# Layer 3's projections in half-array products, the lower half two products behind the upper, and key-value sums four tiles at a time

## The chip, the cores and the metric

The kernel runs on one NeuronCore of a Trainium2 chip. The metric is the device time of one execution in microseconds. TensorE is written PE, its weight loads PEld, VectorE DVE, ScalarE ACT, GpSimd POOL, and SyncE, which issues the DMAs, SP.

## The reference

Four layers run one after the other on x of 2048 tokens by 576 features: a linear attention (A), an MLP (B), the same attention again and the same MLP again. Layers 1 and 3 are A, layers 2 and 4 are B. Each adds its result to x.

```python
def _A_ref(x, wqkv, wo):                 # H = 32 heads of Dh = 18
    qkv = (x @ wqkv) ...                 # q, k, v: 2048 x 576 each
    phi = lambda t: jnp.where(t > 0, t + 1, jnp.exp(t)) + 1e-6
    pq, pk = phi(q), phi(k)
    kv = jnp.einsum("bhsd,bhse->bhde", pk, v)
    z = jnp.einsum("bhsd->bhd", pk)
    num = jnp.einsum("bhqd,bhde->bhqe", pq, kv)
    den = jnp.einsum("bhqd,bhd->bhq", pq, z)[..., None] + 1e-6
    return (num / den) ... @ wo

x = x + _A_ref(_layernorm(x), wqkv, wo)
x = x + _B_ref(_layernorm(x), w1, b1, w2, b2)    # layer norm, 576 -> 4608, gelu, -> 576
x = x + _A_ref(_layernorm(x), wqkv, wo)
x = x + _B_ref(_layernorm(x), w1, b1, w2, b2)
```

## The kernel before, in words

**Tiles.** The 2048 tokens are 16 tiles of 128 (`t`), or four chunks of 512 (`c`). The 576 features are contracted in `KD` = 5 steps of 128 rows, so the fifth step holds 64 real rows; its other 64 rows of `wqkv_sb` are zero. The layer norm's result lies turned in `yT` (features down, tokens across). The 32 heads are in five groups `g` of 126 columns (the last: 72).

**Layer A's projection stage** (`layer_A`, the loop at L486). For each tile it issues:
- `k_proj` (L435): two halves of 288 columns, each five full-array products into a buffer of its own from `ps_h`, then phi. `phi_from_psum` (L375) reads PSUM twice on ACT (exp L381, identity L382) and ends with two DVE operations on SBUF (L383, L385). In layer 3 the second half goes by `phi_by_dve` (L366): exp on ACT (L368), then DVE, whose last operation (L371) reads PSUM too. The result is `pk`.
- `v_proj` (L448): two groups of five products, 252 columns (L454) and 324 columns (L457), into the two banks of one `v_ps` tile under the tag accB. ACT copies both halves' first 252 columns at once (L459), DVE the last 72 (L464; ACT, L462, in the first two tiles), into one of two `v_ring` buffers.
- `kv_acc` (L467) of the tile before: five products that add pk and v into `kvacc`, under the tag accA, over all tiles.
- From tile 2 on (layer 3) one `q_proj` (L475): five products of 512 columns, then phi with the columns turned back into order. Twenty such (g, c) pieces are needed; those left over follow behind the loop and between the output products.

**PSUM.** There are eight banks: `ps_h` has four buffers of one bank; accA and accB are one buffer of two banks each. A tile's buffer is released when all that read it are done.

**Order of the work.** A scheduler orders each engine's instructions; on PE, `pe()` (L141) links every product to the last, so PE's order is the order of the code. Each engine then works its list in order. DMAs are issued by SP in its own order. `pre_a1(t)` gives the layer-norm pipe one tick per tile (`LNPipe.tick`, L276): statistics on DVE, the root on POOL (L309), the norm on DVE into one of three `y_ring` buffers, a DVE transpose, DMAs to DRAM and back into `yT` (`land`, L242). In layer 3 this carries the last tiles of the layer before.

**Half-array products** exist already in layer B (`m1_group`, L625): a product of 64 rows on the upper half of the array and one on the lower half go out in turn. Two halves may not write one PSUM bank at the same time, so a block's first lower product waits for a small copy on ACT (a relay, L671) that waits for its last upper product.

Of the kernel before, what the change touches and what calls it, by code (L numbers as in the profile page):

```python
# [9 lines left out]
BF16 = mybir.dt.bfloat16  # L10
F32 = mybir.dt.float32
PSUM = bass.MemoryType.PSUM
DRAM = bass.MemoryType.DRAM

S, D, F, H, DH = 2048, 576, 4608, 32, 18
P = 128
NT = S // P
KD = 5
DPAD = KD * P
NF = F // P  # L20
G = 5
GH = [7, 7, 7, 7, 4]
GR = [h * DH for h in GH]
GO = [126 * g for g in range(G)]
# [4 lines left out]
CA = 512  # L29
NCA = S // CA  # L30
HALF = D // 2
# [3 lines left out]
def build(tc, A_x, A_wqkv, A_wo, B_w1, B_b1, B_w2, B_b2, out, dbg=None, n_layers=4):  # L35
    nc = tc.nc
    dbg = dbg or {}
    with ExitStack() as ctx:
        const = ctx.enter_context(tc.tile_pool(name="const", bufs=1))
        ps_h = ctx.enter_context(tc.tile_pool(name="ps_h", bufs=4, space=PSUM))  # L40
        ps_acc = ctx.enter_context(tc.tile_pool(name="ps_acc", bufs=1, space=PSUM))
# [57 lines left out]
        wqkv_sb = const.tile([P, KD, 3 * D], BF16, name="wqkv_sb")  # L99
# [6 lines left out]
        yT = const.tile([P, KD, S], BF16, name="yT")  # L106
        kvT = const.tile([P, G, 126], BF16, name="kvT")
        zsel = const.tile([P, G, H], BF16, name="zsel")
        NY = 3
        y_ring = [const.tile([P, DPAD], BF16, name=f"y_ring{i}") for i in range(NY)]  # L110
        NV = 2
        v_ring = [const.tile([P, G, P], BF16, name=f"v_ring{i}") for i in range(NV)]
# [6 lines left out]
        blk = ctx.enter_context(tc.tile_pool(name="blk", bufs=NF))  # L119
# [6 lines left out]

        NOSYNC = mybir.DependencyInfo(mybir.DependencyClass.NoSync, mybir.DependencyReason.SCHED_ONLY)
        SYNC = mybir.DependencyInfo(mybir.DependencyClass.Sync, mybir.DependencyReason.DATA)
        relay_sb = const.tile([P, 2], F32, name="relay_sb")
        nc.gpsimd.memset(relay_sb[:], 0.0)  # L130
        chain = dict(last=None)

# [8 lines left out]
        def pe(inst):  # L141
            if pe_chain["on"]:
                if pe_chain["last"] is not None:
                    tc.add_manual_dep(inst.ins, pe_chain["last"], NOSYNC, reason="TensorE order in the MLP")
                pe_chain["last"] = inst.ins.name
            return inst
# [74 lines left out]
        state = dict(ycnt=0, vcnt=0, turns=0)  # L221
# [20 lines left out]
        def land(now=False):  # L242

            for it in list(landing):
                it[0] -= 1
                if it[0] > 0 and not now:
                    continue
                _, home, c, kind = it
                landing.remove(it)
                cols = slice(c * CB, (c + 1) * CB)  # L250
                nc.sync.dma_start(out=yT[:, 0:KD - 1, cols],
                                  in_=home[0:16, :, :].rearrange("(k jj) r n -> (jj r) k n", jj=4))
                for hi in range(2 if kind == "B" else 1):
                    nc.sync.dma_start(out=yT[64 * hi:64 * (hi + 1), KD - 1, cols],
                                      in_=home[16:18, :, :].rearrange("jj r n -> (jj r) n"))

        def spread(ap):

            return ap.rearrange("p (t i c) -> p i t c", t=TPC, i=4)

        def gather(ap):
            return ap.rearrange("p (i t c) -> p i t c", i=4, t=TPC)

        class LNPipe:
            def __init__(self):
                self.items = []
# [88 lines left out]
            def drain(self):  # L355
                while self.items or landing:
                    self.tick()

        lnp = LNPipe()
        act_last = dict(exp=None, gelu=None)  # L360

        def warm_table(func, after):
            warm = nc.scalar.activation(out=act_dummy[:, 0:1], in_=neg_half[:, 0:1], func=func)
            tc.add_manual_dep(warm.ins, after, NOSYNC, reason="table of the next stage loaded early")
# [10 lines left out]
        def phi_from_psum(ps_ap, out_ap, rows, n, turned_cols=False):  # L375
            e = work.tile([P, 512], BF16, name="phi_e", bufs=3)
            a = work.tile([P, 512], BF16, name="phi_a", bufs=2)
            e_out, a_out = e[0:rows, 0:n], a[0:rows, 0:n]
            if turned_cols:
                e_out, a_out, ps_ap = spread(e_out), spread(a_out), gather(ps_ap)  # L380
            act_last["exp"] = nc.scalar.activation(out=e_out, in_=ps_ap, func=ACT.Exp).ins.name  # L381
            nc.scalar.activation(out=a_out, in_=ps_ap, func=ACT.Identity, bias=C1, scale=1.0)  # L382
            nc.vector.tensor_scalar(out=e[0:rows, 0:n], in0=e[0:rows, 0:n], scalar1=1.0, scalar2=1e-6,  # L383
                                    op0=ALU.min, op1=ALU.add)
            top = nc.vector.tensor_tensor(out=out_ap, in0=a[0:rows, 0:n], in1=e[0:rows, 0:n], op=ALU.max)  # L385
            dve_last["phi"] = top.ins.name
# [42 lines left out]
        def layer_A(li, next_kind, pre_a1=None):  # L429
            kvacc = ps_acc.tile([P, 2, 512], F32, name="kvacc", tag="accA")  # L430
            pk_tiles = {}
            v_tiles = {}
            pq = {}
# [41 lines left out]
            def q_proj(g, c):  # L475
# [5 lines left out]
                pq[(g, c)] = blk.tile([P, D], BF16, name="pq", tag="blk")  # L481
                phi_from_psum(qp[0:GR[g], :], pq[(g, c)][0:GR[g], 0:CA], GR[g], CA, turned_cols=(li > 0))

            q_left = [(g, c) for c in range(NCA) for g in range(G)]
            pe_chain["on"] = True
            for t in range(NT):  # L486
                if t != 1 or li > 0:
                    k_proj(t)
                if t == 0 and li == 0:
                    k_proj(1)  # L490
                pre_a1(t)
                v_proj(t)
                if t >= 1:
                    kv_acc(t - 1)
                if t >= (4 if li == 0 else 2):
                    q_proj(*q_left.pop(0))
# [5 lines left out]
                out=kvT[0:127, 0:4, :].rearrange("p g (h e) -> p g h e", h=7),  # L502
# [3 lines left out]
                out=kvT[0:127, 4, 0:72].rearrange("p (h e) -> p h e", h=4),  # L506
# [3 lines left out]
            for g in range(G):  # L510
                pe(nc.tensor.matmul(zp[0:GR[g], g:g + 1], lhsT=kvT[0:127, g, 0:GR[g]], rhs=z_row[0:127, :],
                                 start=True, stop=True))
# [78 lines left out]
            for t in range(NT):  # L591
                c, j = divmod(t, TPC)
# [17 lines left out]
        def next_acc():  # L610
            acc_turn["n"] += 1
            return ("accA", "accB")[acc_turn["n"] % 2]
# [4 lines left out]
        class LayerB:  # L617
# [69 lines left out]

            def run(self):
                li, next_kind = self.li, self.next_kind

                def feed_next(c, i):
                    if c + 1 < NCB:
                        t = (c + 1) * TPC + i
                        lnp.feed(None, t, "B", "dve", "dma", load_from=t, after=dve_last["sum"])

                for c in range(NCB):
                    for g in range(self.done.get(c, 0), NGRP):
                        self.m1_group(c, g)
                        if g in (3, 5):
                            prefetch_xo(li, c * TPC + (g - 3) // 2, add_b2=True)  # L700
                        if g in (2, 3, 4, 5):
                            feed_next(c, g - 2)
                        lnp.tick(transposes=0)
                        lnp.tick(transposes=0)
                    self.flush()
                    if c == NCB - 1 and next_kind == "A":
                        warm_table(ACT.Exp, act_last["gelu"])
                    hT = self.hT.pop(c)
                    for j in range(TPC):
                        t = c * TPC + j  # L710
                        acc = ps_acc.tile([P, 2, 512], F32, name="m2_ps", tag=next_acc())
                        by_half = li == n_layers - 1 and t == NT - 1
                        steps = [(f, half) for half in range(2) for f in range(NF)] if by_half else \
                            [(f, half) for f in range(NF) for half in range(2)]
                        for f, half in steps:
                            pe(nc.tensor.matmul(acc[:, half, 0:HALF], lhsT=hT[f][:, j * P:(j + 1) * P],  # L716
                                                rhs=w2_sb[:, f, half * HALF:(half + 1) * HALF],
                                                start=(f == 0), stop=(f == NF - 1)))
                            if half == 0:
                                continue  # L720
                            if f % 12 == 6:
                                lnp.tick()
                            if f == 18 and j < 2:
                                prefetch_xo(li, c * TPC + 2 + j, add_b2=True)
                        xn = residual(li, t, acc[:, :, 0:HALF])
                        if xn is not None and next_kind == "A":
                            lnp.feed(xn, t, "A", "dve", "dma")
# [40 lines left out]
        for li, kind in enumerate(kinds):  # L768
            nk = kinds[li + 1] if li + 1 < n_layers else None
            if kind == "A":  # L770
                if li == 0:
                    layer_A(li, nk, pre_a1=pre_a1_layer0)
                else:
                    def pre_a1(t):
                        lnp.tick()
# [56 lines left out]
```

## Time and profile before

| | us |
|---|---|
| median of 3 runs | 778.01 (777.93 to 779.69) |
| the profiled execution | 778.13 |
| its span, first to last instruction | 776.4 |
| PE busy | 765.1 |
| ACT busy | 335.4 |
| DVE busy | 276.4 |
| POOL busy | 119.2 |
| layer 3's projections, 393.4 to 451.9 | 58.5 |

The median and the span are not the same measure: the profiled execution took 1.7 us more than its span. In rows of the timeline the columns are start, duration, engine, line, operation, output and inputs, shape, count, and in brackets the idle time before the row and what ended it. Several instructions of a kind are merged into one row, from the first one's start to the last one's end. In the table by stage the columns are the stretch, its length, and busy time with the number of instructions for PE, PEld, DVE, ACT and POOL, then the granted TensorE clock, the DMA engines' share and GB/s.

### The profile page before, as it was taken

What the parts mean: (1) busy time and instruction counts of PE and PEld (TensorE: products, weight loads), DVE (VectorE), ACT (ScalarE), POOL (GpSimd) and SP (SyncE); (2) the same over time, 40 slices, a digit from 0 to 9 for tenths busy, and PEclk for the clock granted to TensorE, in tenths of its full rate; (3) what the DMA queues carried; (4) which work ended last, traced back from release to release, by engine and by line L of the source; (5) the groups of instructions that cost most, each with busy time, mean ns of one, the idle gap of its engine ahead of it and who ended that gap; (6) DMA issues with size and microseconds to landing.
All of it is one profiled execution on the core that took longest, in us unless ns stands there. A gap on an engine that the chain in (4) does not pass through costs nothing.

```text
span 776.4 us, 15770 instructions
## 1 busy us (share of the span) xinstructions
PE 765.1 (99%) x6613; PEld 495.6 (64%) x6613; DVE 276.4 (36%) x711; ACT 335.4 (43%) x738; POOL 119.2 (15%) x185
## 2 busy tenths in 40 slices
PE   7999999999999999999999999999999999999998
PEld 4777664575477457646777766547745764675476
DVE  5786965045113603400355579520140032000000
ACT  4887746403620660164046675561065026304600
POOL 3573312012000301200100004210030011002000
PEclk9999999999999999999999999999999999999999
DMA  8990374106401720230440006730141033011000
GB/s 268 278 296 22 111 242 121 36 31 171 109 16 48 187 61 32 80 75 2 153 100 9 1 2 208 250 81 8 31 128 53 17 124 80 8 32 54 1 11 21
DMA packets 73761, 69.10 MB, mean 89 GB/s; under 512 B 34266, under 2 KB 58330, under 8 KB 73690
## 3 DMA queue, kind: packets, MB, share of 16 engines
q1 hardware_dynamic: 73690, 68.10, 30.2%
q8 instruction: 51, 0.84, 0.5%
q14 instruction: 20, 0.16, 0.1%
HBM read 45.67 MB, written 22.41 MB: 88 GB/s over the span
## 4 chain that ended last, share of the span: by engine, by line
PE 94%; DVE 3%; ACT 1%; issue 1%; POOL 0%; DVEq 0%; ACTq 0%; POOLq 0%
PE m_ps L716 36%; PE h_ps L666 20%; PE hp_ps L666 16%; PE k_ps L441 5%; PE q_ps L478 5%; PE wo_ps L565 4%; PE v_ps L457 3%; PE v_ps L454 2%; PE kvacc L472 1%; PE tp L346 1%; PE warm_ps L176 1%; PE rden_ps L554 1%; ACT rden_bc L556 1%; DVE pq L557 0%; DVE xn L419 0%
## 5 line engine op out<-in xcount | busy, mean ns | idle before, releaser
L716 PE MATMUL m_ps<-w_sb,hT 128*128 128x288 bf16 x2304 | 283.6, 286 | 0.0
L716 PEld LDWEIGHTS <-hT 128*128 128x128 bf16 x2304 | 224.8, 98 | 59.8 <-issue 3.4
L666 PEld LDWEIGHTS <-w_sb 64*128 64x128 bf16 x2304 | 124.6, 94 | 136.4 <-issue 1.9
L666 PE MATMUL hp_ps<-yT,w_sb 64*128 64x512 bf16 x1152 | 178.0, 376 | 0.0
L666 PE MATMUL h_ps<-yT,w_sb 64*128 64x512 bf16 x1152 | 148.0, 376 | 0.0
L671 ACT COPY relay_sb<-relay_sb 128x1 f32<-128x1 f32 x144 | 28.5, 198 | 264.7 <-PE h_ps L666 222.2
L309 POOL TENSOR_TENSOR ln_rstd<-ln_u,neg_half 128x1 f32<-128x1 f32 x64 | 36.4, 571 | 483.3 <-DVE ln_u L302 253.0
L662 ACT ACTIVATE hT<-h_ps,b1T 128x512 bf16<-128x512 f32 x144 | 91.0, 683 | 44.4 <-PE h_ps L666 44.4
L662 ACT ACTIVATE hT<-hp_ps,b1T 128x512 bf16<-128x512 f32 x144 | 91.1, 692 | 0.0
L419 DVE TENSOR_TENSOR xbf<-m_ps,xo 128x576 bf16<-128x576 f32 (+1 forms) x17 | 12.2, 721 | 221.4 <-PE m_ps L716 221.4
L419 DVE TENSOR_TENSOR xo<-m_ps,xo 128x576 f32<-128x576 f32 x16 | 12.1, 757 | 180.1 <-PE m_ps L716 180.1
L403 POOL TENSOR_TENSOR xo<-xo,b_bc 128x576 f32<-128x576 f32 x32 | 40.9, 1281 | 101.9 <-DMA xo<-x_d 61.5
L666 PE MATMUL h_ps<-yT,w_tail 64*128 64x512 bf16 x144 | 54.2, 376 | 0.0
L666 PE MATMUL hp_ps<-yT,w_tail 64*128 64x512 bf16 x144 | 54.1, 376 | 0.0
L478 PE MATMUL q_ps<-yT,wqkv_sb 128*126 128x512 bf16 (+1 forms) x200 | 50.0, 382 | 0.0
L565 PE MATMUL wo_ps<-kvwo,pq 126*128 126x288 bf16 (+1 forms) x320 | 43.5, 285 | 2.6 <-DVE xo L419 1.5
L441 PE MATMUL k_ps<-wqkv_sb,yT 128*128 128x288 bf16 x320 | 44.3, 286 | 0.0
L565 PEld LDWEIGHTS <-pq 126*128 126x128 bf16 (+1 forms) x320 | 30.4, 97 | 13.7 <-issue 3.5
L441 PEld LDWEIGHTS <-yT 128*128 128x128 bf16 x320 | 31.0, 98 | 11.4
L666 PEld LDWEIGHTS <-w_tail 64*128 64x128 bf16 x288 | 27.1, 94 | 17.1
L383 DVE TENSOR_SCALAR phi_e<-phi_e 128x288 bf16<-128x288 bf16 (+2 forms) x88 | 26.1, 297 | 25.0 <-ACT phi_e L381 24.9
L381 ACT ACTIVATE phi_e<-k_ps 128x288 bf16<-128x288 f32 x48 | 20.2, 420 | 34.2 <-PE k_ps L441 34.1
(98 smaller groups left out, 631.6 us busy)
## 6 DMA issues: line engine op xcount, KB each, us to landing
xo<-x_d SPq DMA_DIRECT2D x48, 288.0 KB, 3.9
x_d<-xo SPq DMA_DIRECT2D x32, 288.0 KB, 2.3
xl<-x_d SPq DMA_DIRECT2D x24, 288.0 KB, 4.3
y_d<-turned SPq DMA_DIRECT2D x40, 144.0 KB, 3.2
w_sb<-in_B_w_dram SPq DMA_DIRECT2D x6, 864.0 KB, 10.2
yT<-y_d SPq DMA_DIRECT2D x10, 512.0 KB, 4.1
w_sb<-in_B_w_dram SPq DMA_DIRECT2D x9, 512.0 KB, 5.4
x_d<-xn SPq DMA_DIRECT2D x16, 288.0 KB, 2.1
```

The lines of the kernel that those rows point to most:

```text
L309: nc.gpsimd.tensor_tensor(out=rstd[:], in0=it["u"][:], in1=neg_half[:], op=ALU.pow)
L383: nc.vector.tensor_scalar(out=e[0:rows, 0:n], in0=e[0:rows, 0:n], scalar1=1.0, scalar2=1e-6, op0=ALU.min, op1=ALU.add)
L403: nc.gpsimd.tensor_tensor(out=xo[:], in0=xo[:], in1=b2_bc[:], op=ALU.add)
L419: total = nc.vector.tensor_tensor(out=xn[:, cols].rearrange("p (h n) -> p h n", h=nh), in0=ps, in1=xo[:, cols].rearrange("p (h n) -> p h n ...
L441: pe(nc.tensor.matmul(kp[:, 0:HALF], lhsT=yT[:, k, tok], rhs=wqkv_sb[:, k, D + half * HALF: D + (half + 1) * HALF], start=(k == 0), stop=( ...
L457: pe(nc.tensor.matmul(vp[:, 1, 0:324], lhsT=yT[:, k, tok], rhs=wqkv_sb[:, k, 2 * D + 252: 3 * D], start=(k == 0), stop=(k == KD - 1)))
L478: pe(nc.tensor.matmul(qp[0:GR[g], :], lhsT=wqkv_sb[:, k, GO[g]:GO[g] + GR[g]], rhs=yT[:, k, c * CA:(c + 1) * CA], start=(k == 0), stop=(k ...
L565: pe(nc.tensor.matmul(wp[:, half, 0:HALF], lhsT=pq[(g, c)][0:GR[g], j * P:(j + 1) * P], rhs=kvwo[g][0:GR[g], half * HALF:(half + 1) * HALF ...
L662: act_last["gelu"] = nc.scalar.activation(out=to, in_=ps, func=ACT.Gelu_apprx_tanh, bias=b1T[:, f:f + 1], scale=1.0).ins.name
L666: mm = pe(nc.tensor.matmul(dst[n], lhsT=wt, rhs=mv, start=(seen[n] == 0), stop=(seen[n] == 8)))
L671: relay = nc.scalar.copy(out=relay_sb[:, 1:2], in_=relay_sb[:, 0:1])
L716: pe(nc.tensor.matmul(acc[:, half, 0:HALF], lhsT=hT[f][:, j * P:(j + 1) * P], rhs=w2_sb[:, f, half * HALF:(half + 1) * HALF], start=(f == ...
```

## The change

It concerns layer 3 alone (li > 0), apart from a weight load ahead of it.

- A job is one output half or piece: v0 (252 columns), v1 (324), k0, k1 (288 each) and q (512). Each tile adds the jobs q (from tile 2), v0, v1, k0, k1. A job has four upper products (rows 0 to 63 of each 128) and four lower ones; the fifth step, 64 rows, is one product more: on the lower half for v0, v1 and k0, on the upper for k1 and q.
- `RowTiles.add` issues a job's upper products; the lower products of the job two before are queued and put between them, as two counters of columns keep the halves level. A job's first lower product waits for a POOL memset (the relay), which waits for its last upper product. When its last lower product is issued, its copies or phi follow.
- The v tile is one accB buffer with two banks as before (for tile 0, two `ps_h` buffers); its copies by ACT and DVE come when both halves are done.
- `kv_acc`, still in full-array products, comes in groups of four tiles behind tiles 4, 8 and 12, then for tiles 12 to 14 behind the loop. Five v buffers are used: the two of `v_ring` and the three of `y_ring`, whose constant columns POOL sets at tiles 1 to 3.
- The layer-norm pipe gets two ticks per tile, ahead of the tile's products.
- The fifth step's 64 rows of keys' and values' weights are loaded a second time into rows 64 to 127, at the start of layer 2, and `yT`'s last 64 rows too for layer 3, by one more DMA per chunk.
- Behind the loop one q, the sums of tile 15 and another q follow as before.

The core of the diff:

```diff
-                for hi in range(2 if kind == "B" else 1):
+                for hi in range(2):
                     nc.sync.dma_start(out=yT[64 * hi:64 * (hi + 1), KD - 1, cols],
...
+                def v_start(half):
+                    def start():
+                        if t == 0:
+                            tiles[half] = ps_h.tile([P, 512], F32, name="v0_ps", tag="h")[...]
+                        else:
+                            if half == 0:
+                                tiles["v"] = ps_acc.tile([P, 2, 512], F32, name="v_ps", tag="accB")
+                            tiles[half] = tiles["v"][:, half, 0:edges[half + 1] - edges[half]]
...
+                def v_finish(half):
+                    def finish():
...
+                        elif half == 1:
+                            nc.scalar.copy(out=va[:, 0:4, 0:126]..., in_=tiles["v"][:, :, 0:252]...)
+                        if half == 1:
+                            nc.vector.tensor_copy(out=va[:, 4, 0:72], in_=tiles[1][:, 252:324])
...
+            class RowTiles:
+                def ops(self, job, hi):
+                    r = slice(64 * hi, 64 * hi + 64)
+                    return [(job, hi, job["w"](r, k), job["m"](r, k))
+                            for k in range(KD - 1 + (job["tail"] == hi))]
+                def emit(self, op, first, last):
+                    job, hi, w, m = op
+                    mm = pe(nc.tensor.matmul(job["dst"], lhsT=w, rhs=m, start=(first and hi == 0), stop=(last and hi == 1)))
+                    self.at[hi] += job["n"]
+                    if first and hi == 1:
+                        tc.add_manual_dep(mm.ins, job["relay"], SYNC, ...)
+                    if last and hi == 0:
+                        relay = nc.gpsimd.memset(relay_sb[:, 2:3], 0.0)
+                        tc.add_manual_dep(relay.ins, mm.ins.name, SYNC, ...)
+                        job["relay"] = self.relay = relay.ins.name
+                    if last and hi == 1:
+                        job["finish"]()
+                def lower(self, limit):
+                    while self.low and (limit is None or self.at[1] <= limit):
+                        self.emit(*self.low.pop(0))
+                def add(self, job):
+                    if len(self.begun) == 2:
+                        if not self.low:
+                            self.at[1] = max(self.at)
+                        self.queue_lower(self.begun.pop(0))
+                    self.begun.append(job)
+                    job["dst"] = job["start"]()
+                    ops = self.ops(job, 0)
+                    for i, op in enumerate(ops):
+                        self.lower(self.at[0] - 1)
+                        self.emit(op, i == 0, i == len(ops) - 1)
+                def full(self, func):
+                    func()
+                    self.at = [max(self.at)] * 2
...
+            if li > 0:
+                va_ring = v_ring + [... for y in (y_ring[(state["ycnt"] + i) % NY] for i in range(NY))]
+                stream = RowTiles()
+                for t in range(NT):
+                    pre_a1(t)
+                    pre_a1(t)
+                    if t in (1, 2, 3):
+                        va = va_ring[t + 1]
+                        for part, value in ((va[:, 4, 72:126], 0.0), (va[:, :, 126:127], 1.0), (va[:, :, 127:128], 0.0)):
+                            init = nc.gpsimd.memset(part, value)
...
+                    if t >= 2:
+                        stream.add(q_job(*q_left.pop(0)))
+                    for job in half_jobs(t):
+                        stream.add(job)
+                    if t % 4 == 0 and t > 0:
+                        stream.full(lambda: [kv_acc(u) for u in range(t - 4, t)])
+                stream.drain()
+                for u in range(NT - 4, NT - 1):
+                    kv_acc(u)
...
             def run(self):
                 li, next_kind = self.li, self.next_kind
+                if next_kind == "A":
+                    nc.sync.dma_start(out=wqkv_sb[64:P, 4, D:3 * D], in_=A_wqkv[4 * P:D, D:3 * D])
```

More of the change, by code (lines that the diff above doesn't have):

```diff
@@ L128, in build @@
         SYNC = mybir.DependencyInfo(mybir.DependencyClass.Sync, mybir.DependencyReason.DATA)
[L129 removed]
+        relay_sb = const.tile([P, 4], F32, name="relay_sb")
         nc.gpsimd.memset(relay_sb[:], 0.0)
@@ L482, in q_proj, with half_jobs, k_start, start @@
                 phi_from_psum(qp[0:GR[g], :], pq[(g, c)][0:GR[g], 0:CA], GR[g], CA, turned_cols=(li > 0))
+            def half_jobs(t):
+                tok = slice(t * P, (t + 1) * P)
+                tiles = {}
+                va = va_ring[t % len(va_ring)]
+                edges = (0, 252, D)
+                def v_start(half):
+                    def start():
+                        if t == 0:
+                            tiles[half] = ps_h.tile([P, 512], F32, name="v0_ps", tag="h")[:, 0:edges[half + 1] - edges[half]]
+                        else:
+                            if half == 0:
+                                tiles["v"] = ps_acc.tile([P, 2, 512], F32, name="v_ps", tag="accB")
+                            tiles[half] = tiles["v"][:, half, 0:edges[half + 1] - edges[half]]
+                        return tiles[half]
+                    return start
+                def v_finish(half):
+                    def finish():
+                        if t == 0:
+                            nc.scalar.copy(out=va[:, 2 * half:2 * half + 2, 0:126],
+                                           in_=tiles[half][:, 0:252].rearrange("p (g c) -> p g c", g=2))
+                        elif half == 1:
+                            nc.scalar.copy(out=va[:, 0:4, 0:126].rearrange("p (b g) c -> p b g c", b=2),
+                                           in_=tiles["v"][:, :, 0:252].rearrange("p b (g c) -> p b g c", g=2))
+                        if half == 1:
+                            nc.vector.tensor_copy(out=va[:, 4, 0:72], in_=tiles[1][:, 252:324])
+                            v_tiles[t] = va
+                    return finish
+                def k_start(half):
+                    def start():
+                        tiles["k", half] = ps_h.tile([P, 512], F32, name="k_ps", tag="h")[:, 0:HALF]
+                        if half == 0:
+                            tiles["pk"] = blk.tile([P, D], BF16, name="pk", tag="blk")
+                        return tiles["k", half]
+                    return start
+                def k_finish(half):
+                    def finish():
+                        phi = (phi_from_psum, phi_by_dve)[half]
+                        phi(tiles["k", half], tiles["pk"][:, half * HALF:(half + 1) * HALF], P, HALF)
+                        if half == 1:
+                            pk_tiles[t] = tiles["pk"]
+                    return finish
+                def rows_of(cols):
+                    return lambda r, k: wqkv_sb[r, k, cols]
+                y_of = lambda r, k: yT[r, k, tok]
+                jobs = []
+                for half in range(2):
+                    cols = slice(2 * D + edges[half], 2 * D + edges[half + 1])
+                    jobs.append(dict(w=y_of, m=rows_of(cols), tail=1, n=edges[half + 1] - edges[half],
+                                     start=v_start(half), finish=v_finish(half)))
+                for half in range(2):
+                    cols = slice(D + half * HALF, D + (half + 1) * HALF)
+                    jobs.append(dict(w=y_of, m=rows_of(cols), tail=1 - half, n=HALF,
+                                     start=k_start(half), finish=k_finish(half)))
+                return jobs
@@ new lines, in q_job, with start, finish @@
+            def q_job(g, c):
+                hold = {}
+                def start():
+                    hold["q"] = ps_h.tile([P, 512], F32, name="q_ps", tag="h")[0:GR[g], :]
+                    return hold["q"]
+                def finish():
+                    pq[(g, c)] = blk.tile([P, D], BF16, name="pq", tag="blk")
+                    phi_from_psum(hold["q"], pq[(g, c)][0:GR[g], 0:CA], GR[g], CA, turned_cols=True)
+                return dict(w=lambda r, k: wqkv_sb[r, k, GO[g]:GO[g] + GR[g]],
+                            m=lambda r, k: yT[r, k, c * CA:(c + 1) * CA], tail=0, n=CA, start=start, finish=finish)
@@ new lines, in layer_A, with __init__, queue_lower, drain @@
+            class RowTiles:
+                def __init__(self):
+                    self.at = [0, 0]
+                    self.begun = []
+                    self.low = []
+                def ops(self, job, hi):
[7 more added lines that the diff above has]
+                    if first and hi == 1:
+                        tc.add_manual_dep(mm.ins, job["relay"], SYNC, reason="row tiles take turns on a PSUM bank")
+                    if last and hi == 0:
+                        relay = nc.gpsimd.memset(relay_sb[:, 2:3], 0.0)
+                        tc.add_manual_dep(relay.ins, mm.ins.name, SYNC, reason="row tiles take turns on a PSUM bank")
+                        job["relay"] = self.relay = relay.ins.name
[4 more added lines that the diff above has]
+                        self.emit(*self.low.pop(0))
+                def queue_lower(self, job):
+                    ops = self.ops(job, 1)
+                    self.low += [(op, i == 0, i == len(ops) - 1) for i, op in enumerate(ops)]
+                def add(self, job):
[12 more added lines that the diff above has]
+                    self.at = [max(self.at)] * 2
+                def drain(self):
+                    while self.begun:
+                        self.queue_lower(self.begun.pop(0))
+                    self.lower(None)
@@ L484, in layer_A @@
             q_left = [(g, c) for c in range(NCA) for g in range(G)]
             pe_chain["on"] = True
-            for t in range(NT):
-                if t != 1 or li > 0:
+            if li > 0:
+                va_ring = v_ring + [y[:].rearrange("p (g c) -> p g c", g=G) for y in
+                                    (y_ring[(state["ycnt"] + i) % NY] for i in range(NY))]
+                stream = RowTiles()
[3 more added lines that the diff above has]
+                    if t in (1, 2, 3):
+                        assert t < 3 or not lnp.busy()
+                        va = va_ring[t + 1]
+                        for part, value in ((va[:, 4, 72:126], 0.0), (va[:, :, 126:127], 1.0), (va[:, :, 127:128], 0.0)):
+                            init = nc.gpsimd.memset(part, value)
+                            tc.add_manual_dep(init.ins, stream.relay, NOSYNC, reason="relays first")
+                    if t >= 2:
[7 more added lines that the diff above has]
+                    kv_acc(u)
@@ L488, in layer_A @@
+            for t in range(NT if li == 0 else 0):
+                if t != 1:
                     k_proj(t)
-                if t == 0 and li == 0:
+                if t == 0:
                     k_proj(1)
```

## The prediction

> **What bounds the kernel now.** I read the page first: TensorE is busy for nearly the whole span at the full granted clock, and the chain of work that ended last is TensorE.
>
> ```profile
> span 776.4 us, 15770 instructions
> PE 765.1 (99%) x6613; PEld 495.6 (64%) x6613; DVE 276.4 (36%) x711; ACT 335.4 (43%) x738; POOL 119.2 (15%) x185
> ...
> PE 94%; DVE 3%; ACT 1%; issue 1%; POOL 0%; DVEq 0%; ACTq 0%; POOLq 0%
> ```
>
> So the change is worth what it does to TensorE's products and waits in one stage, layer 3's projections. The table by stage cuts it out: from the first k_ps product (393.42) to the first q_ps product behind the token loop (451.93) it is 58.5 us, all of it PE, while ACT is busy for 38.4 and DVE for 33.1.
>
> ```profile
> 393.40:451.90 58.50, 58.50 (x467) 44.26 (x465) 33.09 (x112) 38.35 (x92) 0.55 (x1) 1.00 0.13 32
> ```
>
> The timeline of PE over one token tile shows products back to back. A row is a run of products: its length less that of one, over the count less one, is the step from product to product.
>
> ```profile
> 423.20 0.85 PE L457 MATMUL v_ps<-wqkv_sb,yT 128*128 128x324 bf16 x5
> 423.89 0.42 PE L472 MATMUL kvacc<-pk,v_ring 128*128 128x126 bf16 x5
> 424.15 1.26 PE L478 MATMUL q_ps<-yT,wqkv_sb 128*126 128x512 bf16 x5
> 425.25 1.39 PE L441 MATMUL k_ps<-wqkv_sb,yT 128*128 128x288 bf16 x10
> 426.48 0.70 PE L454 MATMUL v_ps<-wqkv_sb,yT 128*128 128x252 bf16 x5
> ```
>
> With one product's 271, 286 and 300 ns (252, 288, 324 columns) the steps are 107, 122.5 and 137.5 ns; 512 columns take 216. One tile with q is 3.81 us (k_ps at 425.25 and, a tile earlier, 421.44).
>
> **The gain: fewer products.** The MLP already works in half-array products. Its timeline gives their step: from one w_tail row to the next like it lie 18 half products, nine pairs, in 1.94 us, so a pair takes 215.6 ns, as long as one full product.
>
> ```profile
> 265.13 0.38 PE L666 MATMUL h_ps<-yT,w_tail 64*128 64x512 bf16 x1
> ...
> 267.07 0.38 PE L666 MATMUL h_ps<-yT,w_tail 64*128 64x512 bf16 x1
> ```
>
> I give each half product the step of the full product of its width. Per tile, in emitted order:
> - upper: v0 4x107 = 0.43, v1 4x137.5 = 0.55, k0 4x122.5 = 0.49, k1 5x122.5 = 0.61, q 5x216 = 1.08: together 3.16 us (7,456 columns);
> - lower, beside them: k1 of the tile before 4x122.5 = 0.49, q 4x216 = 0.86, v0 5x107 = 0.54, v1 5x137.5 = 0.69, k0 5x122.5 = 0.61: together 3.19 us (7,520 columns).
>
> The lower half is the longer one: 14 tiles with q at 3.19 and two without at 2.33 are 49.3 us, and it starts 0.98 late, behind two upper products. Key-value sums stay what they were: 15 tiles at 0.275 (five products, the row at 423.89 up to 424.15) are 4.1.
>
> Going between full and half products costs something, and the MLP's edges price it. The last half product starts at 357.82 and the first full one at 358.12, in exact starts 308 ns against the usual 216: 92 ns. The other way, the fourth L716 product of the run from 322.47 starts at 322.84 and the half product at 323.05, 217 against 122.5: 95 ns.
>
> ```profile
> 322.47 0.65 PE L716 MATMUL m_ps<-w_sb,hT 128*128 128x288 bf16 x4
> 323.05 0.61 PE L666 MATMUL h_ps<-yT,w_sb 64*128 64x512 bf16 x4
> ...
> 357.82 0.38 PE L666 MATMUL hp_ps<-yT,w_tail 64*128 64x512 bf16 x1
> 358.12 0.42 PE L716 MATMUL m_ps<-w_sb,hT 128*128 128x288 bf16 x2
> ```
>
> There are four of each (at the start, around three groups of sums, at the end): 0.75 us. Sum without waits: 0.98 + 49.3 + 4.1 + 0.75 = 55.2, that is 3.3 us less than 58.5.
>
> **The loss: the single v buffer.** Both halves of v_ps share the one accB buffer, and the first upper product of the next v must wait until both copies of the last one are done. Today q_ps, k_ps and kvacc lie between, and nothing waits. The price of a release stands in the timeline of ACT and DVE:
>
> ```profile
> 424.09 0.58 ACT L459 CAST v_ring<-v_ps 128x504 bf16<-128x504 f32 x1 [0.46 <-PE v_ps L457]
> 424.70 0.23 DVE L464 CAST v_ring<-v_ps 128x72 bf16<-128x72 f32 x1 [0.31 <-ACT v_ring L459]
> ```
>
> The last L457 product starts at 423.75, the DVE copy waits for ACT's and ends at 424.93. From a copy's end to the waiting PE is another 0.05, and that such a wait stops PE is seen where layer 1 has no q to lie between:
>
> ```profile
> 12.03 0.23 ACT L462 CAST v_ring<-v_ps 128x72 bf16<-128x72 f32 x1
> ...
> 12.31 0.70 PE L454 MATMUL v_ps<-wqkv_sb,yT 128*128 128x252 bf16 x5 [0.51 <-ACT v_ring L462]
> ```
>
> So a release takes 1.23 us from the start of v1's last product. After the change, count from the start of a tile's v0. The lower v1's last product starts at 0.49 + 0.86 + 0.54 + 4x0.1375 = 2.44. The next v0 is due at 3.16. That leaves 0.72 and wants 1.23: PE stands for 0.51. Behind the waiting product stands the lower k1, so both halves stand. The lower half also falls behind by 64 columns (27 ns) a tile, which its counters never make up, as its queue is never empty; v1 ends later by that much each tile. From 0.51 to about 0.86 over 14 tiles, 0.69 in the mean: 9.6 us. Bounds: nothing if PE could go on past the wait, and 14 x 0.95 = 13.3 if each copy starts 0.26 later behind other work. I take 9.6, since at that moment ACT's two passes over q are just over, and k0's have not begun.
>
> A second wait is small. The four ps_h buffers turn by three a tile, so q takes the one of k1 two tiles earlier. Its chain is product 0.29, handover 0.04 (424.05 to 424.09), exp start to the end of DVE's L371 1.21 (423.19 to 424.40), 0.05 to PE: 1.59. The time there is: k1's last lower product starts at 0.37, the next q is due at 2.08, which leaves 1.71 and shrinks by 27 ns a tile. From about the fifth tile it is short, by 0.1 in the mean for nine tiles: 0.9 us, between 0 and 3 (0.2 more per tile if DVE is busy).
>
> **At nothing:** the relays. Upper end to POOL, a 0.10 memset (L130's row) and 0.05 to PE, with 0.04 (PE to ACT) to 0.15 (DVE to POOL at L309) for the handover, is 0.5 to 0.65 from the last upper product's start; the lower one is due 0.70 to 1.2 later. POOL works for 0.55 us in this stage, one L309, which can delay one relay by 0.1 or so. The ring memsets come behind relays, when the layer norms are through; at worst one POOL wait of 1 us. The two ticks a tile move layer norm and yT's last rows earlier, and PE needs those only at tile 12. The added DMAs (64 rows of wqkv_sb, one more yT piece for four chunks) fall into the MLP, where SP and the DMA engines have slack (29% share from 111.5 to 393.4); without that cover they cost up to 0.5 us of SP issue each (L254 at 263.58 took 0.52). At the stage's end k1's chain of 1.7 us has sums and a q, 2.0 us, before the last kvacc.
>
> **Sum:** -3.3 + 9.6 + 0.9 = +7.2. The profiled execution took 778.13 (span 776.4 and 1.7 around it), 0.12 above the median: 785.3 either way.
>
> **Rivals.**
> - *Products of unequal width hold each other.* The MLP pairs 512 with 512 alone; here 252 to 324 run beside 512. If a product may not end before an earlier one, a short one beside a q waits for up to (512-288)/2.4 = 93 ns, nine times a tile, 0 to 0.84 us; starts laid out in order give 0.13, so +1.8 in 14 tiles: 787.1, at most 790 with a longer q wait. The Trainium skill, "TensorE: Matmul & The Clock Gate", Part 3 (Packing small matmuls), states that matmuls start and end strictly in program order; by it the time would be this rival's, and no row here has unequal pairs to show it. Chance 0.13. That halves do not overlap at all the MLP's pairs speak against.
> - *Relays come late:* POOL takes 1.3 instead of 0.6; +3: 788.3. Chance 0.06.
> - *Half the wait:* the DVE copy no longer waits for ACT's, release 0.97: 0.26 less in 14 tiles, 781.7. Against it: L464's row, released by ACT. Chance 0.06.
> - *Nearly even:* the wait shrinks to 0.24 a tile and cancels the gain: 778. Chance 0.07.
> - *Faster: a waiting upper product does not hold the lower half.* Then lower products run on by the 0.5 to 0.9 us that the release lacks, v1 ends that much sooner, and the gain of 3.3 stands: 774.8. It decides once the lower half gets about 0.5 us ahead. Against it: PE at 12.31 started nothing while it waited. Chance 0.08.
>
> **Numbers.** The forecast has 0.60, with 783.5 to 788 as its own spread. The range 780.5 to 790.5 takes in the first three rivals and leaves out the even and the faster one (0.15). A difference under 0.3% (2.3 us) can't be told from none here: faster 0.08, the same 0.07, slower 0.85.
>
> **What would show it.** In layer 3's stage: an idle stretch of PE of 0.5 to 0.9 us before every first v_ps product, released by DVE's v_ring copy; small ones before q_ps, released by DVE's pk; a stage of about 65.7 us. No idle before v_ps means the faster rival; steps above 216 or 122.5 within runs mean the unequal pairs; idle released by relay_sb means POOL.

## The result, and the profile after

The changed kernel takes 788.60 us (787.93 to 789.25, four runs) against 778.72 for the kernel before beside it: a ratio of 1.0126, with a 95% interval from 1.0114 to 1.0138. The forecast was 785.3 in a range of 780.5 to 790.5. The profiled executions differ by 9.8 us (787.93 and 778.13). The times of each kernel lie at two levels, 1.3 to 1.8 us apart (787.9 and 789.2 here, 777.9 and 779.5 before), which go with the granted clock told of in the last section.

The page of the changed kernel, the same three lines as before:

```profile
span 785.8 us, 16566 instructions
PE 765.7 (97%) x6925; PEld 499.6 (64%) x6925; DVE 280.0 (36%) x713; ACT 337.7 (43%) x737; POOL 128.0 (16%) x272
...
PE 92%; DVE 3%; ACT 3%; issue 1%; POOL 1%; DVEq 0%; POOLq 0%; ACTq 0%
```

PE is busy for as long as before; the span is 9.4 us longer. In the chain that ended last, ACT's part is now 3% instead of 1% and POOL's 1% instead of 0%. The table by stage for layer 3's projections, from the first half product (393.48) to the first full q_ps product (461.18), shows where:

```profile
393.50:461.20 67.70, 59.17 (x779) 48.36 (x779) 36.18 (x115) 41.40 (x93) 9.22 (x88) 1.00 0.12 29
```

It is 67.7 us against 58.5, and PE stands for 8.5 us of it by its recorded ends. What follows up to layer 4 takes 38.9 us against 39.0, so the loss is in this stage. Who waited for whom (us in all, times, longest) names it:

```profile
PE v_ps L573 <- DVE y_ring L510: 4.4, 9, 0.7
...
PE v_ps L573 <- DVE v_ring L510: 2.4, 5, 0.6
```

Fourteen stops ahead of v_ps, all ended by the DVE copy L510 (five v buffers: two named v_ring, three y_ring). One of them, in the timeline of PE, ACT and DVE:

```profile
419.35 0.43 PE L573 MATMUL v_ps<-wqkv_sb,yT 64*128 64x324 bf16 x2
419.54 0.38 PE L573 MATMUL q_ps<-yT,wqkv_sb 64*126 64x512 bf16 x1
...
419.97 0.38 PE L573 MATMUL q_ps<-yT,wqkv_sb 64*126 64x512 bf16 x1
419.99 0.28 PE L573 MATMUL k_ps<-wqkv_sb,yT 64*128 64x288 bf16 x1
420.86 0.26 PE L573 MATMUL v_ps<-wqkv_sb,yT 64*128 64x252 bf16 x1 [0.51 <-DVE v_ring L510]
420.86 0.29 PE L573 MATMUL k_ps<-wqkv_sb,yT 64*128 64x288 bf16 x1
```

```profile
419.96 0.58 ACT L507 CAST v_ring<-v_ps 128x504 bf16<-128x504 f32 x1 [0.29 <-PE v_ps L573]
```

```profile
420.57 0.23 DVE L510 CAST v_ring<-v_ps 128x72 bf16<-128x72 f32 x1 [0.45 <-ACT v_ring L507]
```

The last lower product of v1 starts at 419.49 (the second of the row at 419.35) and is followed by ACT's copy, DVE's copy and, 0.06 us later, the next v0. The lower k_ps product (k0's fifth), which waits for nothing itself, starts only with it. The bracket says 0.51, but the last product, q_ps at 419.97, was due to be followed 0.216 later, at 420.19: in steps PE stood for 0.67. A recorded idle time of PE is short of the stop by some 0.165 us, because a product's recorded end lies that far behind the moment at which the next could start. Below, a stop is counted in steps.

Over all tiles the release, from v1's last product to the next v0, is 1.23 us in eleven cases and 1.32 to 1.37 in three, ahead of tiles 6 to 8. The example is one of the three. ACT had been idle for 0.29 when its copy began, so it was not ACT that was late. The copy starts 0.04 us after the recorded end of the q product at 419.54 (419.92), as it elsewhere starts 0.04 after the end of v1's last product (here 419.78). By the order of the code this q product is issued just ahead of v1's last one; it started 0.05 later and, being wider, ended later. In the three cases v1's last product thus counted as done only when the q product ahead of it was, 0.09 to 0.14 late. No run was made to test this reading.

The stops are 0.48 at tiles 2 to 5, 0.61 to 0.72 at 6 to 12 and 0.85 at 13 to 15: 9.1 us.

A second loss is at the start, on POOL:

```profile
396.24 0.55 POOL L309 TENSOR_TENSOR ln_rstd<-ln_u,neg_half 128x1 f32<-128x1 f32 x1 [0.90 <-PE v_ps L573]
396.74 0.10 POOL L578 MEMSET relay_sb<- 128x1 f32 x1
396.77 0.14 POOL L626 MEMSET y_ring<- 128x54 bf16 x1
398.28 0.16 POOL L626 MEMSET y_ring<- 128x5 bf16 x2 [1.36 <-DVE turned L230]
398.35 0.27 POOL L578 MEMSET relay_sb<- 128x1 f32 x2
```

```profile
396.90 0.29 PE L573 MATMUL k_ps<-wqkv_sb,yT 64*128 64x288 bf16 x1 [0.32 <-POOL relay_sb L578]
...
398.51 0.28 PE L573 MATMUL v_ps<-wqkv_sb,yT 64*128 64x252 bf16 x1 [0.94 <-POOL relay_sb L578]
```

A relay stands behind the layer norm's root, and the next behind a constant memset that waits for DVE's transpose. The two stops are 0.48 and 1.10 in steps.

The stage adds up, in us:

| | forecast | measured |
|---|---|---|
| products and sums, with no stop or switch | 54.4 | 55.1 (what is left) |
| eight switches between half and full | 0.75 | 0.75 |
| stops ahead of v0 | 9.6 | 9.1 |
| stops ahead of q | 0.9 | 1.1 |
| stops for relays | 0 | 1.6 |
| stage | 65.7 | 67.7 |

### The profile page after: what moved, and what is told of

It is laid out like the page before. It is cut to its first block, busy times and chain, and to the rows that moved or that the text cites. A ratio compares the mean times of both kernels' runs of the same rounds, so it can differ in the third digit from the quotient of the medians.

```text
span 785.8 us, 16566 instructions
## 1 busy us (share of the span) xinstructions
PE 765.7 (97%) x6925; PEld 499.6 (64%) x6925; DVE 280.0 (36%) x713; ACT 337.7 (43%) x737; POOL 128.0 (16%) x272
## 4 chain that ended last, share of the span: by engine, by line
PE 92%; DVE 3%; ACT 3%; issue 1%; POOL 1%; DVEq 0%; POOLq 0%; ACTq 0%
PE m_ps L869 36%; PE h_ps L817 20%; PE hp_ps L817 16%; PE wo_ps L716 3%; PE v_ps L573 3%; PE q_ps L478 2%; PE k_ps L441 2%; PE k_ps L573 2%; PE q_ps L573 1%; PE v_ps L457 1%; PE kvacc L472 1%; PE v_ps L454 1%; PE tp L346 1%; PE warm_ps L176 1%; ACT y_ring L507 1%
## 5 line engine op out<-in xcount | busy, mean ns | idle before, releaser
L573 PEld LDWEIGHTS <-yT 64*128 64x128 bf16 x576 | 39.4, 94 | 17.9 <-issue 9.1
L573 PE MATMUL v_ps<-wqkv_sb,yT 64*128 64x252 bf16 (+1 forms) x288 | 41.5, 282 | 7.8 <-DVE y_ring L510 4.4
L573 PE MATMUL k_ps<-wqkv_sb,yT 64*128 64x288 bf16 x288 | 42.3, 283 | 0.3 <-POOL relay_sb L578 0.3
L383 DVE TENSOR_SCALAR phi_e<-phi_e 126x512 bf16<-126x512 bf16 (+2 forms) x88 | 26.4, 300 | 21.7 <-ACT phi_e L381 21.1
L478 PE MATMUL q_ps<-yT,wqkv_sb 128*126 128x512 bf16 (+1 forms) x130 | 32.5, 382 | 0.0
```

Source lines behind the costliest of these rows:

```text
L478: pe(nc.tensor.matmul(qp[0:GR[g], :], lhsT=wqkv_sb[:, k, GO[g]:GO[g] + GR[g]], rhs=yT[:, k, c * CA:(c + 1) * CA], start=(k == 0), stop=(k ...
L573: mm = pe(nc.tensor.matmul(job["dst"], lhsT=w, rhs=m, start=(first and hi == 0), stop=(last and hi == 1)))
```

## The experiments

The theory: the release of the joint v tile sets the stage's pace. Rivals: products of unequal width hold each other; the switches or the relays are the price; something else in the change (order, grouped sums, layer norm) costs. "Before" is the kernel before, run beside each.

**One held tile, banks copied apart.**

```diff
-                            if half == 0:
-                                tiles["v"] = ps_acc.tile([P, 2, 512], F32, name="v_ps", tag="accB")
+                            if "v" not in v_hold:
+                                v_hold["v"] = ps_acc.tile([P, 2, 512], F32, name="v_ps", tag="accB")
+                            tiles["v"] = v_hold["v"]
...
-                        if t == 0:
+                        if True:
                             nc.scalar.copy(out=va[:, 2 * half:2 * half + 2, 0:126],
```

> One v tile held for the whole stage, its two banks copied out apart (ACT copies each half when that half is done), so a bank is free for the next v0 as soon as its own half is copied. Theory (the v buffer's release sets the stage): the 14 stops ahead of v0, 6.9 us as recorded and some 9.2 from product to product, vanish; 788.6 - 9.2 = 779.4 us, and about 0.8 us of q stops remain. Rival (half products of unequal width, or the switches around the sums, make the stage long, and the v wait only takes up slack that would show elsewhere): 786 us or more, with idle or longer steps at other products.

Measured: 797.42 us, ratio 1.0262 (1.0238 to 1.0287); the stage 77.0. Neither theory nor rival: there are 28 stops ahead of v products instead of 14, 17.0 us in steps instead of 9.1. In the timeline:

```profile
423.52 0.36 ACT L507 CAST v_ring<-v_ps 128x252 bf16<-128x252 f32 x1
...
423.93 0.29 PE L576 MATMUL v_ps<-wqkv_sb,yT 64*128 64x324 bf16 x1 [0.71 <-ACT v_ring L507]
```

v1's first lower product now waits for the copy of v0 in the other bank of the same tile. The wait is kept for the tile as a whole; the edit added one per tile instead of taking one away. It did not test the theory, but it shows that nothing hides a stop here: 7.9 us more of them came with a stage that is 9.3 longer (the other 1.4 were not taken apart).

**One held tile, copies as they were.** Only the first hunk above.

> The same held tile, but the copies as in the changed kernel (ACT copies both halves' 252 columns at once, DVE the last 72 behind it). Bank 0 is then free after ACT's copy, without DVE's 0.03 + 0.23 us. Theory: the release falls from 1.23 to 0.97 us, 0.26 less at each of 14 stops: 788.6 - 3.6 = 785.0 us, and the stops are ended by ACT. Rival (the price of the release does not matter): 788.6.

Measured: 788.09 us, ratio 1.0135 (1.0120 to 1.0150); the stage 67.70, as in the changed kernel, and the same 14 stops, still ended by DVE. For the same reason the release was not shortened, so the run leaves the expected 0.26 per stop untried.

**The ring turned by one.**

```diff
-                                    (y_ring[(state["ycnt"] + i) % NY] for i in range(NY))]
+                                    (y_ring[(state["ycnt"] + 1 + i) % NY] for i in range(NY))]
```

> The three y_ring buffers are taken one place further, so that the first one POOL fills is not the one that the last layer norm is about to use. Theory: POOL's constant memsets no longer wait for the last transpose on DVE, the relay behind them comes about 1.1 us sooner, and the longer of the two stops at the stage's start (0.94 us recorded, at 398.5) goes: 787.5 us. Rival (the relays' delay is hidden by what follows): 788.6.

Measured: 788.31 us, ratio 1.0130 (1.0113 to 1.0147); the stage 67.4 against 67.7. The 0.94 is gone, but a new stop stands in its place:

```profile
PE k_ps L573 <- DVE v_ring L510: 0.5, 1, 0.5
```

DVE's copy of the first v, which frees a ps_h buffer, stands behind the layer norm's last operations. So 0.3 came of 1.1: the next thing was late as well.

**Both.**

> The held tile with banks copied apart and the ring turned by one. Theory: the two effects add, 788.6 - 9.2 - 1.1 = 778.3 us, equal to the kernel before within its spread. Rival (unequal products or switches): 785 us or more.

Measured: 796.56 us, ratio 1.0239 (1.0224 to 1.0255), the stage 76.6: the first edit's two stops per tile again, less the 0.4 of the ring.

**Two tiles for v.** accB's pool is closed for the stage and its two banks are given to two tiles.

```diff
+                ps_acc.close()
+                ps_acc.open("ps_v")
                 stream = RowTiles()
...
-                            if half == 0:
-                                tiles["v"] = ps_acc.tile([P, 2, 512], F32, name="v_ps", tag="accB")
-                            tiles[half] = tiles["v"][:, half, 0:edges[half + 1] - edges[half]]
+                            tiles[half] = ps_acc.tile([P, 512], F32, name="v_ps", tag=("v0", "v1")[half])[:, 0:edges[half + 1] - edges[half]]
...
-                        if t == 0:
+                        if True:
                             nc.scalar.copy(out=va[:, 2 * half:2 * half + 2, 0:126],
```

> The two banks of v become two tiles of their own (v0, v1), each copied out when its own half is done and released alone; accB's two banks are given to them for this stage. The held tile of the runs before left its waits whole-tile, so it did not test this. Theory (the release of the joint v tile sets the stage): v0's last lower product starts 1.78 us into the tile, its copy is through 0.7 later, well ahead of 3.16, so the 14 stops (9.2 us from product to product) go; v1 may be short by 0.1 or 0.2 in the late tiles, 0.5 in all. 788.3 - 9.2 + 0.5 = 779.6 us. Rival (unequal half products, switches or added waits make the stage long whatever the v buffer does): 785 or more.

Measured: 779.55 us, ratio 1.0016 (1.0006 to 1.0025); the stage:

```profile
393.40:452.60 59.20, 57.49 (x779) 48.93 (x779) 35.99 (x115) 41.86 (x108) 9.43 (x88) 1.00 0.13 33
```

59.2 us against 67.7. The products and their order are the same; the joint release is gone, and ACT copies each half by itself. That is 8.5 us in the stage, 9.1 in the medians. What is left ahead of v is 0.7 in steps, at v1. The theory holds, and the rivals that would have kept 785 fall.

**Two tiles, the ring turned, all keys' phi by ACT.** To the last kernel and the turned ring comes:

```diff
-                        phi = (phi_from_psum, phi_by_dve)[half]
+                        phi = phi_from_psum
```

> As v_two_tiles, with the ring turned by one (0.3 us in its own run) and the second half of keys also by exp and identity on ACT, so that its bank is released 0.5 us sooner and the q stops (0.75 us) go; ACT gets 0.3 us more per tile, in a stage where it is busy for 60%. Theory: 779.6 - 0.3 - 0.8 = 778.5 us, the kernel before within its spread. If ACT becomes the bound: 781 or more, with ACT busy all along the stage.

Measured: 778.27 us, ratio 1.0000 (0.9992 to 1.0009), the stage 57.8; no stop ahead of q is left, and ACT is busy for 46.0 of 57.8, so it is not the bound.

**Full-array products, the rest kept.**

```diff
                 def add(self, job):
-                    if len(self.begun) == 2:
...
                     job["dst"] = job["start"]()
-                    ops = self.ops(job, 0)
...
+                    for k in range(KD):
+                        pe(nc.tensor.matmul(job["dst"], lhsT=job["w"](slice(0, P), k), rhs=job["m"](slice(0, P), k),
+                                            start=(k == 0), stop=(k == KD - 1)))
+                    job["finish"]()
```

The second copy of the weights' last rows is not loaded, and the memsets of the v buffers' constant columns are no longer ordered behind a relay.

> Keys, values and queries again in full-array products (no lower half, no relays, no second copy of the weights' last rows); the rest of the change stays: order q, v, k, sums in groups of four, five v buffers, two ticks a tile. Theory (the loss lies in the half products' waits alone): v1's last product lies k0, k1 and q ahead of the next v0, 2.3 us against a release of 1.23, no stop; 778 us, within 1 of the kernel before. Rival (grouping the sums or moving the layer norm costs): 780 or more.

Measured: 778.17 us, ratio 0.9999 (0.9990 to 1.0008):

```profile
393.20:451.50 58.30, 58.30 (x468) 44.27 (x466) 35.33 (x115) 40.94 (x93) 0.92 (x5) 1.00 0.13 33
```

58.3 us, PE never idle. The order of the jobs, the sums by four and the two ticks cost nothing; the loss belongs to the half products and what they wait for.

**One product behind.**

```diff
-                    if len(self.begun) == 2:
+                    if len(self.begun) == 1:
```

> The lower half follows one product behind the upper, not two. Theory: the v stops go, as v1's lower products lie beside k0 and the next v0 is k1 and q away; but each lower start must wait for its relay, which comes 0.49 us behind the last upper product's start (393.81 to POOL's memset at 394.15, then 0.1 and 0.06), one upper product after it: 0.27 to 0.38 us of stop at each of 78 products, 27 us; 788.3 - 10 + 27 = 805 us. Rival (the relay is quick enough, the second product of lag is needless): 780.

Measured in one execution: 782.04 us, 778.32 before; the stage 62.0. Faster than two behind, as the v stops shrink from 9.1 to some 3.0 us, but nowhere near 805. The mistake: I took each lower start one upper product behind its relay's cause. The lower half's queue never runs empty, so its products come later than they are queued. Relays stop PE nine times, for 2.9 us in steps: six times in the first three tiles, then three times by 0.2 to 0.3. Neither the theory of 27 us nor a needless second product holds.

**The start by ACT.** To two_tiles_ring_phi come: the first eight relays and the first two tiles' 72-column copies by ACT; the memsets of tile 1 on a v buffer are no longer ordered behind a relay.

```diff
+                            if t < 2:
+                                nc.scalar.copy(out=va[:, 4, 0:72], in_=tiles[1][:, 252:324])
...
+                        if self.relays <= 8:
+                            relay = nc.scalar.copy(out=relay_sb[:, 3:4], in_=relay_sb[:, 0:1])
```

> As two_tiles_ring_phi, and at the stage's start the first eight relays and the first two tiles' 72-column copies go by ACT, so that neither stands behind POOL's root or DVE's layer norm. Theory (what is left of stops lies there: 0.32 and 0.51 us recorded, some 0.7 and 0.5 of it gained after ACT's own queue): 778.3 - 1.1 = 777.2 us, faster than both kernels by 0.1%. Rival (ACT's phi of the first keys stands ahead of a relay, and the stops only change their name): 778.3.

Measured: 776.35 us, ratio 0.9972 (0.9963 to 0.9981): 0.28% less than the kernel before, with an interval that leaves out 1. Its profile is of an execution of 1623.45 us, so the stage is read from a second one:

> The kernel of act_start once more, for a profile at the full granted clock: in its first profiled execution every TensorE step took twice its time. Theory: 776.3 us; the stage 55.7 to 56.5 us against 57.8 in two_tiles_ring_phi, with no stop of more than 0.3 us at its start. If the gain came from elsewhere, the stage is 57.8 as before.

It took 777.54 us (778.49 before, beside it), with the stage

```profile
394.80:451.30 56.50, 56.50 (x779) 48.61 (x779) 33.36 (x113) 46.89 (x134) 8.53 (x77) 1.00 0.14 35
```

56.5 us, 1.3 less than two_tiles_ring_phi, with no recorded idle of PE. So the half products are worth 2.1 us here once nothing stops them.

**Sums behind every tile.** two_tiles_ring_phi with

```diff
-                    if t % 4 == 0 and t > 0:
-                        stream.full(lambda: [kv_acc(u) for u in range(t - 4, t)])
+                    if t > 0:
+                        stream.full(lambda: [kv_acc(u) for u in range(t - 1, t)])
```

> As two_tiles_ring_phi, but the key-value sums of a tile go right behind the next tile, 15 times instead of in three groups of four. Theory (each change between half and full products costs 95 and 92 ns, 0.19 a pair): 12 more pairs, 778.3 + 2.2 = 780.5 us, 0.2 to 0.5 more if pk is late for its sums. Rival (the switches are covered, grouping is needless): 778.3.

Measured: 789.31 us, ratio 1.0135 (1.0117 to 1.0153), the stage 68.2 against 57.8: 10.4 us, where the twelve more pairs of switches alone give 2.2; the steps show them at 0.093 to 0.095 into half products and 0.092 back. Most of the rest is v again:

```profile
PE v_ps L587 <- DVE y_ring L524: 2.0, 6, 0.4
PE v_ps L587 <- DVE v_ring L524: 1.0, 3, 0.4
```

By the code, after each group both column counters are set level while the lower half still has its queue, so it falls further behind: from tile 9 on all of v0's lower products lie beside q (mostly beside k1 with sums by four). So v1 ends later, and the release of v1's own tile is missed as well. In steps the v stops are 4.9 us and pauses within the sums 1.7; the remaining 1.6 I did not take apart (halves running alone are my reading, not shown by a run).

## Why the prediction was right, and where it was off

- **The mechanism was right.** Each first v0 product waited for the v copies, ended by DVE, with both halves standing. The release was 1.23 as worked out from the trace of before (eleven of 14), the stops 0.48 to 0.85 where 0.51 to 0.86 were forecast, 9.1 us in all instead of 9.6. They grew in steps, not by 27 ns a tile. Giving v two tiles took nearly all of them away.
- **The gain was too large by 0.7.** 54.4 us of products without stops stand against 55.1. The sum took the lower half as the longer one throughout; at its ends and where unlevel halves meet a switch, one half works alone. This is read from the sum, not shown apart.
- **The switches** cost what the MLP's edges showed: 0.093 to 0.095 into half products, 0.092 back.
- **The second wait** (q behind keys' phi) was 1.1 instead of 0.9, in the late tiles, as the lower half falls back.
- **The step that failed is "at nothing: the relays".** It allowed one relay a delay of 0.1 and ring memsets at worst 1 us, and put 0 into the sum. Measured are two stops of 0.48 and 1.10, released by relay_sb, the sign that the prediction named for POOL. The relays' own time was right (the first: product at 393.81, memset at 394.15 for 0.10, 0.06 to PE); what stood ahead of them on POOL was not: I took the layer norms to be through by then, but `va_ring` counts from the buffer that the last layer norm is about to use. ring_turn, which takes another buffer first, does away with the 1.10 but not with the 0.48 behind the root.
- **Outside the stage** the changed kernel takes 0.4 more around the span. That is no spread: time less span is 2.1 to 2.2 in all four of its executions, 1.7 to 1.8 in those of the kernel before, and 1.7 to 1.8 in ring_turn's; what makes it, no run shows. The 0.2 more after layer 3 lies within what the other kernels show there.
- **The total is near the wrong rival.** 788.60 lies above the forecast's own spread (783.5 to 788) and beside the 788.3 of "relays come late". But that rival had POOL take 1.3 instead of 0.6 us, and here two relays at the start make 1.6 us of stops; the rest of the miss is in the products, the q stops and outside the stage, less 0.5 at v. That its figure fits is luck.
- **Unequal products do not hold each other's steps.** Within a run 252 columns go on at 0.107 and 288 at 0.122 beside 512 at 0.216 (419.11, 419.32, 419.54, 419.76, 419.97 for q), so that rival's 1.8 us of longer steps did not come. The Trainium skill ("TensorE: Matmul & The Clock Gate", Part 3, Packing small matmuls) states that matmuls start and end strictly in program order; in this trace v1's last product starts at 419.49, ahead of the q product at 419.54 that is issued before it, so for the starts the measurement decides. For the ends the trace agrees: the three late releases above, 0.09 to 0.14 us each, are as if v1's last product had to end behind that q product. This part of the rival was right, at 0.4 us in all.
- **A waiting upper product does hold the lower half,** against the faster rival: at 420.86 the free k_ps product starts with the one that waited.

## What to carry to other kernels

When a product is spread over two halves that follow one another, its PSUM buffer is held longer, while the time until its next use shrinks: work out, for each buffer, the time from its last product to its release (with every copy behind it, and the handovers) against the time to its next first product. In these runs a wait was kept for the tile: what shall be free apart must be a tile of its own. A relay on an engine that also serves other work is only as quick as what stands ahead of it in that engine's order.

## What the runs showed of the hardware

PE's granted clock fell to half for 3.4 us in layer 1 in three of the twelve profiled executions that have clock records (v_release_by_act, ring_turn and act_start_again), and not in the nine others. Before it, PE waits for 2.54 to 2.66 us from 15 us on in all twelve; what decides between the two, no run shows. Here is the same stretch of the kernel before and of ring_turn, columns as in the table by stage:

```profile
18.50:22.00 3.50, 3.50 (x36) 2.87 (x35) 1.30 (x4) 2.67 (x7) 2.47 (x5) 1.00 0.92 277
```

```profile
18.50:22.00 3.50, 3.50 (x21) 2.29 (x19) 0.47 (x2) 1.49 (x4) 2.37 (x4) 0.53 0.94 288
```

21 products instead of 36 at a clock of 0.53. Layer 3's projections then begin at 394.8 to 395.2 in the three executions, 393.2 to 393.8 in the nine. So a difference near 1 us between two kernels is better read from a stage than from single times.
